# Windowed attention with two gated networks on one core: q laid out with the four head pairs innermost, and its stationary operand read with a step of 4

## The chip, the cores and the metric

The kernel runs on one core of a Trainium2 chip. The metric is the device time of one execution in microseconds. Most executions of one kernel agree within some tenths of a per cent.

## The reference

Three parts follow each other. The first is attention over 4 batches, 8 heads, 576 positions and head dimension 64, in which each query sees itself and the 63 keys before it:

```python
scores = scale * np.matmul(q, k.transpose(0, 1, 3, 2))
mask = (rel >= 0) & (rel < 64)              # rel = query position - key position
attn = softmax(np.where(mask, scores, -1e9))
x = attn @ v                                # heads side by side: (4, 576, 512)
```

The second adds to x the real part of a two-dimensional Fourier transform of x, normalises each row, and adds a network of width 2048 with a ReLU. The third is a gated network of width 1024 with a GELU, whose gate is normalised and mixed over the positions by a 576 by 576 matrix. Everything is float32 in and out.

## The kernel before, in words

**Stages.** Attention runs first, in blocks of 64 queries of all 8 heads (36 blocks: 9 in each of 4 batches). The Fourier transform and the normalisation of the first batches (`dft`, `ln`) and the decoding of the first weights (`decode_f`) are woven into it. Then come the ReLU network (`mlp`), with the rest of the transform beside it, and the gated network (`gate_u`, `v_tiles`, `spatial`, `project`). Later stages use matmuls in three terms (`mm3`, lines 113 to 120) of operands of 128 by 128 and 128 by 256 or 320.

**A block of attention.** `scores` (line 254) computes four products, one for each pair of heads, of a 128 by 128 stationary operand from q and 128 keys from k. The stationary operand of a pair has the 64 dimensions of one head on partitions 0 to 63 and those of the other on partitions 64 to 127; its 128 columns are 64 queries of the first head and 64 of the second, and the two off-diagonal quarters are zero. Each such float32 matmul is two loads of the stationary operand and two matmuls in the trace, so that 36 blocks of 4 pairs make 288 of each. VectorE adds the mask and takes the maximum (line 264), GpSimd and ScalarE make the exponential, `transposes` (line 277) turns the block by PE, `pv` multiplies by v, `norm` divides, and `xt` (line 317) turns the result into `uT`. A block's transposes come one block behind its scores, pv two behind, xt three behind (`LAG`).

**Where q lives.** Three tiles `qring` (line 196) serve as a ring; each holds two blocks. The zero quarters are written once, by 6 memsets on VectorE and 6 on GpSimd (lines 199 and 200). `load_q` (line 211) fills the other quarters: one DMA for each half of the partitions, 64 partitions each, for two blocks at a time (for one block in the first two and in the last of a batch). In the tile a partition's row is (block, head pair, half, query), so that 64 queries of a head, 256 bytes, stand together, and the other half's zeros stand between them.

**Queues.** All loads but those of the Fourier tables are issued by SP, in the order that `load_attn` (line 235) gives them: q, then k of three blocks, then v. `load_attn(n + 4)` follows the scores of block n. At the start SP issues the q and k of block 0, the mask, the q of block 1, the q of blocks 2 and 3, the v of block 0, and then the k of blocks 3 to 5. A load waits until the matmuls that read its buffer before are done, and what stands behind it on SP waits as well.

**Order of the work.** The lanes that are woven into attention advance by written costs (`drive`, line 734). A planner with its own estimates of each instruction's duration then orders the instructions of each engine; the order is fixed when the program is built.

Of the kernel before, what the change touches and what calls it, by code (L numbers as in the profile page):

```python
# [9 lines left out]
F32 = mybir.dt.float32  # L10
# [7 lines left out]
B, H, S, D = 4, 8, 576, 64  # L18
DM, FF, FG = 512, 2048, 1024
NB = S // 64  # L20
# [17 lines left out]
UB, SB, QB, VB = 3, 3, 3, 3  # L38
# [16 lines left out]
def tables():  # L55
    d = np.arange(256.0)[:, None]
    dp = np.arange(258)
    ang = 2 * np.pi * ((d * dp) % 512) / 512
    cd = np.cos(ang)
    cd[0] = 1 - dp % 2  # L60
    cd[:, 257] = 0
    sd = np.sin(ang)[:, :256]
    sd[(d[:, 0:1] * dp[:256] % 256) == 0] = 0
    t = np.arange(289.0)[:, None]
    tp = np.arange(290)
    ang = 2 * np.pi * ((t * tp) % 576) / 576
    cs = np.cos(ang)
    cs[288] *= 0.5
    cs[:, 289] = 0
    ss = np.sin(ang)  # L70
    ss[(t * tp) % 288 == 0] = 0
    ss[:, 289] = 0
    out = []
    for m in (cd, sd):
        for p in split(m):
            out.append(p.reshape(2, 128, -1).transpose(1, 0, 2).reshape(128, -1))
    g = np.zeros((128, 258), np.float32)
    g[0] = g[32] = dp % 2
    g[:, 257] = 0
    out.append(g)  # L80
    for m in (cs, ss):
        hi, lo = split(m)
        th = np.zeros((128, 3, 290), np.float32)
        th[:, 0], th[:, 1], th[:33, 2], th[64:97, 2] = hi[:128], hi[128:256], hi[256:], hi[256:]
        tl = np.zeros((128, 3, 290), np.float32)
        tl[:, 0], tl[:, 1], tl[:33, 2] = lo[:128], lo[128:256], lo[256:]
        out += [th.reshape(128, -1), tl.reshape(128, -1)]
    return np.ascontiguousarray(np.concatenate(out, 1))


def masks():
    q = np.arange(64)[:, None]
    k = np.arange(64)[None]
    m = np.zeros((2, 64, 2, 64), np.float32)
    m[:, :, 0] = np.where(k > q, 0, -8e9)
    m[:, :, 1] = np.where(k <= q, 0, -8e9)
    m0 = m.copy()
    m0[:, :, 0] = -8e9
    return np.ascontiguousarray(np.stack([m.reshape(128, 128), m0.reshape(128, 128)], 1))


class Kernel:
# [86 lines left out]
    def open_attn(self):  # L189
        nc = self.nc  # L190
        self.ap_, self.attn_es = self.pool("attn", side="right")
        p = self.ap_
        self.aps_, es = self.pool("attn_ps", side="right", space=PSUM)
        self.attn_es.enter_context(es)
        self.mask = p.tile([128, 2, 128], F32, name="mask")
        self.qring = [p.tile([128, 2, 4, 2, 64], F32, name=f"q{i}") for i in range(QB)]
        for t in self.qring:
            for i in range(2):
                nc.vector.memset(t[0:64, i, :, 1], 0.0)
                nc.gpsimd.memset(t[64:128, i, :, 0], 0.0)  # L200
        self.qt = {}
        self.kt, self.vt = {}, {}

# [7 lines left out]
    def load_q(self, b, j, w):  # L211

        t, o = self.qring[(b * 5 + j // 2) % QB], j % 2
        for h in range(2):
            dst = t[64 * h:64 * h + 64, o:o + w, :, h].rearrange("d n a q -> d (n a) q")
            self.nc.sync.dma_start(dst, self.aps["q"][b, h, :, j:j + w].rearrange("d n a q -> d (n a) q"))
        for i in range(w):
            self.qt[b, j + i] = t[:, o + i]

    def load_v(self, b, j):  # L220

# [27 lines left out]
    def attention(self):  # L249
        nc, p, ps = self.nc, self.ap_, self.aps_  # L250
# [3 lines left out]
        def scores(n):  # L254
            b, j = divmod(n, NB)
            q, k = self.qt.pop((b, j)), self.kt[b, j // 3]
            sc = ps.tile([128, 4, 128], F32, tag="sc", bufs=2, name="sc")
            for hp in range(4):
                o = 64 * (j % 3)
                nc.tensor.matmul(sc[:, hp], lhsT=q[:, hp].rearrange("p a b -> p (a b)"), rhs=k[:, hp, o:o + 128], start=True, stop=True)  # L260
            mx = p.tile([128, 4], F32, tag="mx", bufs=3, name="mx")
            s = p.tile([128, 4, 128], F32, tag="s", bufs=SB, name="s")
            for hp in range(4):
                nc.vector.tensor_tensor_reduce(
                    out=s[:, hp], in0=sc[:, hp], in1=self.mask[:, int(j == 0)], scale=1.0, scalar=-3e38,
                    op0=ALU.add, op1=ALU.max, accum_out=mx[:, hp:hp + 1])
            if n % XP[0] >= XP[1]:
                nc.gpsimd.tensor_tensor(out=s, in0=s, in1=mx[:].unsqueeze(2).to_broadcast([128, 4, 128]), op=ALU.subtract)
                nc.scalar.activation(out=s, in_=s, func=AF.Exp, scale=0.125)
            else:  # L270
                nm = p.tile([128, 4], F32, tag="nm", bufs=3, name="nm")
                nc.gpsimd.tensor_scalar(out=nm, in0=mx, scalar1=-0.125, scalar2=None, op0=ALU.mult)
                for hp in range(4):
                    nc.scalar.activation(out=s[:, hp], in_=s[:, hp], func=AF.Exp, bias=nm[:, hp:hp + 1], scale=0.125)
            st[n] = s
# [61 lines left out]
        for n in range(N + LAG[2] + 1):  # L337
            if n in TAB_AT:
                self.load_tables(TAB_AT.index(n))
            if n < N:  # L340
                scores(n)
            self.load_attn(n + 4)
            if n < N:
                yield 870
            m = n - LAG[0]
            if 0 <= m < N:
                transposes(m)
                yield 440
            m = n - LAG[1]
            if 0 <= m < N and full(m):  # L350
                pv(m)
                yield 1800 if m % NB % 2 else 900
                norm(m)
            m = n - LAG[2]
            if 0 <= m < N and full(m):
                xt(m)
                yield 440
# [548 lines left out]
def layout(q, k, v, w1, w2, w_in, g, w_sg, b_sg, w_out):  # L906
    ca = np.ascontiguousarray
    ho = list(ORDER)
    o = {}
    o["q"] = ca(q[:, ho].reshape(B, 4, 2, NB, 64, D).transpose(0, 2, 5, 3, 1, 4))  # L910
    kt = np.zeros((B, 128, 4, 64 + S), np.float32)
    kt[:, :, :, 64:] = k[:, ho].reshape(B, 4, 2, S, D).transpose(0, 2, 4, 1, 3).reshape(B, 128, 4, S)
    o["k"] = kt
    vt = np.zeros((B, 64 + S, 8, 65), np.float32)
    vt[:, :, :, 64] = 1
    vv = v[:, ho].transpose(0, 2, 1, 3)
    vt[:, 64:, 0:4, 0:64] = vv[:, :, 0:4]
    vt[:, 64:, 4:8, 0:64] = vv[:, :, 4:8, ::-1]
    o["v"] = vt.reshape(B, 64 + S, 520)
    w = lambda a: ca(a).view(np.int64)  # L920
    o["w1"] = w(w1[SIGMA].reshape(4, 128, NF, 128).transpose(2, 1, 0, 3)).reshape(NF, 128, 512)
    o["w2"] = w(w2[:, SIGMA]).reshape(NF, 128, 512)
    o["wi"] = w(w_in[SIGMA].reshape(4, 128, 2, 512).transpose(2, 0, 1, 3)).reshape(8, 128, 512)
    o["wo"] = w(w_out[:, SIGMA]).reshape(4, 128, 512)
    st = w_sg.T
    o["sg"] = ca(np.concatenate([st[:256], st[320:], st[256:320], st[256:320]]).reshape(5, 128, S))
    o["g"] = ca(g.reshape(4, 128).T)
    o["b"] = ca(b_sg.reshape(1, S))
    o["tab"] = tables()
    o["mask"] = masks()  # L930
    return o
# [20 lines left out]
```

## Time and profile before

| | |
|---|---|
| median of three runs | 819.7 us (814.97 to 820.48) |
| the profiled execution | 818.62 us, of which the span of its instructions is 816.9 us |
| TensorE (PE) busy | 785.6 us, 96% of the span |
| VectorE (DVE) busy | 486.1 us, 60% |
| ScalarE (ACT) busy | 278.0 us, 34% |
| GpSimd (POOL) busy | 194.6 us, 24% |
| DMA packets | 59322, of which 22384 under 512 bytes |
| granted TensorE clock, mean | 0.99 |

PE stands for matmuls and PEld for the loads of their stationary operands, which go on beside matmuls. Busy time is the time in which at least one instruction of the engine is under way. A matmul's duration contains its way through the array, so that consecutive ones overlap in time; the pace of a group is read from its whole length and its count. DMA is the busy share of the core's 16 DMA engines. [...]

### The profile page before, as it was taken

How to read it: one execution, taken by the hardware profiler on the slowest of the kernel's cores; microseconds unless marked ns; L12 is line 12 of the kernel's file. 1: busy time of each engine (PE TensorE's matmuls, PEld its weight loads, DVE VectorE, ACT ScalarE, POOL GpSimd, SP SyncE). 2: the span in 40 equal slices, each digit the busy share in tenths (PEclk: the TensorE clock that was granted, in tenths of full speed). 3: DMA queues.
4: the chain of work that ended last, by engine and by line, in shares of the span. 5: the costliest groups of instructions: out<-in, count | busy, mean ns of one | idle time of the engine just before them, and what ended most of it. 6: DMA issues, size and time to landing. Idle time of an engine off the chain costs nothing. (4 is left out here: it accounts for less than half of the span.)

```text
span 816.9 us, 15597 instructions
## 1 busy us (share of the span) xinstructions
PE 785.6 (96%) x6084; PEld 754.2 (92%) x6084; DVE 486.1 (60%) x1390; ACT 278.0 (34%) x638; POOL 194.6 (24%) x238
## 2 busy tenths in 40 slices
PE   7979789899999999999999999999999999999998
PEld 6869678799998999999999999999999998989898
DVE  3678988997478547972235933653240267565753
ACT  2655565443233224431113411333233243131310
POOL 3464746343032003420002300232251020010000
PEclk9989999999999999999999999999999999999999
DMA  8996641122002002430001400122131010303032
GB/s 232 307 274 188 172 136 44 39 92 78 1 28 78 1 1 79 130 104 1 1 1 53 130 26 1 33 89 94 59 103 42 1 53 8 117 1 117 1 116 93
DMA packets 59322, 63.71 MB, mean 78 GB/s; under 512 B 22384, under 2 KB 42736, under 8 KB 59248
## 3 DMA queue, kind: packets, MB, share of 16 engines
q1 hardware_dynamic: 58672, 59.75, 25.2%
q0 software_dynamic: 576, 2.97, 1.2%
q8 instruction: 48, 0.79, 0.4%
q14 instruction: 26, 0.21, 0.1%
HBM read 53.25 MB, written 9.44 MB: 77 GB/s over the span
## 5 line engine op out<-in xcount | busy, mean ns | idle before, releaser
L118 PE MATMUL acc<-rh,set 128*128 128x256 f32 (+1 forms) x512 | 151.5, 296 | 2.3 <-DVE uT L555 2.2
L118 PE MATMUL h<-xh,set 128*128 128x256 f32 (+1 forms) x512 | 151.2, 296 | 1.2 <-DVE rl L575 1.2
L119 PE MATMUL acc<-rl,set 128*128 128x256 f32 (+1 forms) x512 | 151.3, 296 | 0.0
L120 PE MATMUL acc<-rh,set 128*128 128x256 f32 (+1 forms) x512 | 151.1, 295 | 0.0
L119 PE MATMUL h<-xl,set 128*128 128x256 f32 (+1 forms) x512 | 151.0, 295 | 0.0
L120 PE MATMUL h<-xh,set 128*128 128x256 f32 (+1 forms) x512 | 150.9, 295 | 0.0
L160 POOL TENSOR_TENSOR set<-dec_w,set 128x256 fp32r<-128x256 f32 x88 | 70.8, 810 | 242.4 <-ACT set L159 238.9
L575 DVE SCALAR_TENSOR_TENSOR rl<-h,rh 128x320 fp32r<-128x320 f32 (+1 forms) x128 | 58.1, 454 | 118.1 <-ACT rh L574 117.5
L574 ACT ACTIVATE rh<-h 128x320 fp32r<-128x320 f32 (+1 forms) x128 | 51.8, 405 | 160.7 <-PE h L120 120.9
L118 PEld LDWEIGHTS acc<-rh,set 128*128 128x128 f32 x512 | 96.4, 188 | 3.9 <-issue 2.3
L118 PEld LDWEIGHTS h<-xh,set 128*128 128x128 f32 x512 | 96.3, 188 | 2.1 <-DVE rl L575 1.8
L120 PEld LDWEIGHTS acc<-rh,set 128*128 128x128 f32 x512 | 96.5, 188 | 0.1
L119 PEld LDWEIGHTS h<-xl,set 128*128 128x128 f32 x512 | 96.4, 188 | 0.1
L120 PEld LDWEIGHTS h<-xh,set 128*128 128x128 f32 x512 | 96.4, 188 | 0.0
L119 PEld LDWEIGHTS acc<-rl,set 128*128 128x128 f32 x512 | 96.4, 188 | 0.0
L555 DVE TENSOR_TENSOR uT<-acc,uT 128x320 f32<-128x320 f32 (+1 forms) x160 | 62.0, 447 | 15.1 <-PE acc L120 15.1
L154 ACT ACTIVATE dec_g<-dec_s 128x256 f32<-128x256 f32 x88 | 38.5, 439 | 76.4 <-DVE dec_w L156 38.8
L488 POOL TENSOR_TENSOR rq<-rq,mhalf 128x1 f32<-128x1 f32 (+2 forms) x26 | 17.4, 670 | 187.5 <-DVE rq L487 184.4
L155 DVE TENSOR_SCALAR dec_w<-dec_s 128x256 int32<-128x256 int32 x88 | 37.4, 428 | 34.6 <-POOL set L160 23.1
L120 PE MATMUL c<-xh,set 128*128 128x256 f32 (+1 forms) x188 | 55.4, 294 | 0.0
L118 PE MATMUL c<-xh,set 128*128 128x256 f32 (+1 forms) x188 | 55.3, 294 | 0.0
L119 PE MATMUL c<-xl,set 128*128 128x256 f32 (+1 forms) x188 | 55.3, 294 | 0.0
(193 smaller groups left out, 1639.6 us busy)
## 6 DMA issues: line engine op xcount, KB each, us to landing
dec_s<-in_w SPq DMA_DIRECT2D x64, 256.0 KB, 2.8
v<-in_v SPq DMA_DIRECT2D x16, 520.0 KB, 5.1
k<-in_k SPq DMA_DIRECT2D x11, 512.0 KB, 7.1
dec_s<-in_wi SPq DMA_DIRECT2D x16, 256.0 KB, 2.7
q<-in_q SPq DMA_DIRECT2D x30, 128.0 KB, 6.1
x<-uT SPq DMA_DIRECT2D x4, 640.0 KB, 3.9
out<-uT SPq DMA_DIRECT2D x4, 640.0 KB, 3.9
dec_s<-in_wo SPq DMA_DIRECT2D x8, 256.0 KB, 2.6
```

Source lines behind the costliest of these rows:

```text
L118: mm(out, lhsT=lh, rhs=rh, start=first and i == 0, stop=False)
L119: mm(out, lhsT=lh, rhs=rl, start=False, stop=False)
L120: mm(out, lhsT=ll, rhs=rh, start=False, stop=last and i == n - 1)
L154: nc.scalar.activation(out=g, in_=s[:, :, 1].bitcast(F32), func=AF.Copy, scale=2.0 ** -112)
L155: nc.vector.tensor_scalar(out=w, in0=s[:, :, 0], scalar1=29, scalar2=None, op0=ALU.logical_shift_right)
L160: (eng or nc.gpsimd).tensor_tensor(out=lo[:, o:o + 256], in0=f, in1=hi[:, o:o + 256], op=ALU.subtract)
L488: self.nc.gpsimd.tensor_tensor(out=y, in0=v, in1=self.mhalf[:m, 0:n], op=ALU.pow)
L555: V.tensor_tensor(out=x, in0=acc[:, c, 0:size], in1=x, op=ALU.add)
L574: A.activation(out=rh, in_=o, func=AF.Relu)
L575: V.scalar_tensor_tensor(out=rl, in0=o, scalar=0.0, in1=rh, op0=ALU.max, op1=ALU.subtract)
```

## The change

The array q in device memory has its last two axes exchanged, so that query comes before head pair. In the tile a partition's row becomes (block, half, query, head pair). A block's data for one partition are then 256 consecutive floats, 1 KB, where there were four runs of 256 bytes. The load moves the same bytes with that shape. The zero quarters become one run of 1 KB for each block, and one memset covers both blocks of a tile: 3 memsets on each engine of twice the size. The stationary operand of head pair `hp` is now every fourth float of the block, from the float `hp` on.

```diff
-        self.qring = [p.tile([128, 2, 4, 2, 64], F32, name=f"q{i}") for i in range(QB)]
+        self.qring = [p.tile([128, 2, 2, 64, 4], F32, name=f"q{i}") for i in range(QB)]
         for t in self.qring:
-            for i in range(2):
-                nc.vector.memset(t[0:64, i, :, 1], 0.0)
-                nc.gpsimd.memset(t[64:128, i, :, 0], 0.0)
+            nc.vector.memset(t[0:64, :, 1], 0.0)
+            nc.gpsimd.memset(t[64:128, :, 0], 0.0)
...
-            dst = t[64 * h:64 * h + 64, o:o + w, :, h].rearrange("d n a q -> d (n a) q")
-            self.nc.sync.dma_start(dst, self.aps["q"][b, h, :, j:j + w].rearrange("d n a q -> d (n a) q"))
+            dst = t[64 * h:64 * h + 64, o:o + w, h].rearrange("d n q a -> d n (q a)")
+            self.nc.sync.dma_start(dst, self.aps["q"][b, h, :, j:j + w].rearrange("d n q a -> d n (q a)"))
         for i in range(w):
-            self.qt[b, j + i] = t[:, o + i]
+            self.qt[b, j + i] = t[:, o + i].rearrange("p h q a -> p (h q) a")
...
-                nc.tensor.matmul(sc[:, hp], lhsT=q[:, hp].rearrange("p a b -> p (a b)"), rhs=k[:, hp, o:o + 128], start=True, stop=True)
+                nc.tensor.matmul(sc[:, hp], lhsT=q[:, :, hp], rhs=k[:, hp, o:o + 128], start=True, stop=True)
...
-    o["q"] = ca(q[:, ho].reshape(B, 4, 2, NB, 64, D).transpose(0, 2, 5, 3, 1, 4))
+    o["q"] = ca(q[:, ho].reshape(B, 4, 2, NB, 64, D).transpose(0, 2, 5, 3, 4, 1))
```

## Rows read from the trace of the kernel before

**Rows 1.** Busy time by stretch: stretch, length, busy us (instructions) of each engine, clock, DMA.
```profile
0.00:20.00 20.00, 14.74 (x97) 13.40 (x98) 6.29 (x46) 5.96 (x13) 7.24 (x23) 0.91 0.88 228
20.00:40.00 20.00, 19.16 (x226) 16.37 (x225) 13.86 (x82) 13.46 (x30) 9.53 (x16) 1.00 1.12 304
40.00:60.00 20.00, 14.77 (x141) 12.61 (x140) 16.21 (x54) 11.10 (x27) 12.95 (x14) 0.83 1.09 282
60.00:140.00 80.00, 70.91 (x724) 62.80 (x723) 69.37 (x260) 45.93 (x107) 44.40 (x51) 0.96 0.50 141
140.00:816.90 676.90, 666.00 (x4906) 648.99 (x4906) 380.35 (x951) 201.60 (x462) 120.51 (x137) 1.00 0.17 53
```

**Rows 2.** What PE waited for, 0 to 60 us: total us, times, longest.
```profile
PE xt L323 <- DVE x L313: 3.3, 1, 3.3
PE sc L260 <- DMA k<-in_k: 2.3, 1, 2.3
...
PE pv L294 <- DMA v<-in_v: 1.2, 1, 1.2
PE sc L260 <- DMA q<-in_q: 0.8, 1, 0.8
```

**Rows 3.** PE in order of time, first 20 us: start, length, instruction, count, idle before.
```profile
5.73 3.30 PE L260 MATMUL sc<-k,q 128*128 128x128 f32 x16
9.81 1.13 PE L260 MATMUL sc<-k,q 128*128 128x128 f32 x8 [0.79 <-DMA q<-in_q]
...
13.69 1.13 PE L260 MATMUL sc<-k,q 128*128 128x128 f32 x8 [2.31 <-DMA k<-in_k]
```

**Rows 4.** DMA queues in three stretches (112.6 to 114.2, 572 to 574, 0 to 60).
```profile
q1 hardware_dynamic: 544, 0.13, 36.3%
...
q1 hardware_dynamic: 375, 0.38, 56.0%
...
q1 hardware_dynamic: 19792, 13.31, 86.0%
q0 software_dynamic: 555, 2.88, 16.5%
...
q<-in_q SPq DMA_DIRECT2D x18, 128.0 KB, 7.9
...
q<-in_q SPq DMA_DIRECT2D x8, 64.0 KB, 5.1
```

**Rows 5.** SP's time to issue one load, minimum/median/maximum in ns, by tile.
```profile
L216 SPq DMA_DIRECT2D q<-in_q x42: 595/622/2002, 0.7 to 111.9; - x42
...
L208 SPq DMA_DIRECT2D k<-in_k x13: 564/630/2329, 2.3 to 96.6; - x13
...
L233 SPq DMA_DIRECT2D v<-in_v x16: 368/485/2815, 6.9 to 127.5; - x16
...
L151 SPq DMA_DIRECT2D dec_s<-in_w x16: 328/407/743, 18.5 to 147.2; - x16
```

**Rows 6.** Instructions by line and shape, 0 to 180 us: busy us, mean ns of one.
```profile
L260 PEld LDWEIGHTS sc<-k,q 128*128 128x128 f32 x288 | 37.9, 207 | 6.6 <-POOL s L268 2.5 <-DVE mx L264 2.2 <-POOL nm L272 0.9
...
L154 ACT ACTIVATE dec_g<-dec_s 128x256 f32<-128x256 f32 x22 | 9.5, 436 | 11.0 <-DVE dec_w L156 8.4 <-DMA dec_s<-in_w 2.5
L159 ACT ACTIVATE set<-dec_w 128x256 fp32r<-128x256 f32 x20 | 8.1, 409 | 4.0 <-DVE dec_w L157 3.8
L118 PEld LDWEIGHTS h<-xh,set 128*128 128x128 f32 x30 | 5.7, 189 | 0.7 <-DVE rl L575 0.7
...
L199 DVE MEMSET q<- 64x256 f32 x6 | 1.6, 272 | 0.9 <-PEq L939 0.8
...
L323 PEld LDWEIGHTS xt<-ident,x 64*128 64x128 f32 x16 | 1.4, 137 | 0.8 <-issue 0.3 <-DVE mx L264 0.2 <-ACT uT L325 0.2
...
L118 PEld LDWEIGHTS g<-tab,eh 128*33 128x33 f32 x6 | 0.7, 109 | 0.0
```

**Rows 7.** One block's scores in order of time, matmuls and loads, at full clock.
```profile
61.84 1.05 PE L260 MATMUL sc<-k,q 128*128 128x128 f32 x8
...
61.73 0.98 PEld L260 LDWEIGHTS sc<-k,q 128*128 128x128 f32 x8
```

## The prediction

> **What bounds the kernel now.** I read the busy time by stretch first. From 140 us on PE works 666.0 of 676.9 us [rows 1]; the change touches nothing there, so what it gains or loses before 140 us arrives at the end as it is. Up to 140 us PE is busy 14.74 + 19.16 + 14.77 + 70.91 = 119.6 us and idle 20.4 us. That idle time is what faster loads can win, and also what can swallow longer work of PE. The list of waits says who causes it in the first 60 us: the DMAs of k, v and q together 2.3 + 1.2 + 0.8 = 4.3 us, VectorE 3.3 us at once [rows 2]. The order in time shows where: the scores of block 3 start at 13.69 us, after 2.31 us of waiting for k, those of block 2 wait 0.79 us for q [rows 3]. In the same stretch the two data queues take 86.0% and 16.5% of the 16 DMA engines [rows 4]: they have no room left, so shorter transfers there can start others sooner. After 60 us DMA is at 0.50 [rows 1], and a shorter transfer buys little.
>
> **The transfers.** In 112.6 to 114.2 us only packets of q were moving: 544 packets took 36.3% of 16 x 1.6 us, which is 17.1 ns for 256 bytes. In 572 to 574 us there were only packets of 1 KB: 375 took 56.0% of 16 x 2 us, 47.8 ns [rows 4]. So 1 KB of q costs 4 x 17.1 = 68.3 ns now and 47.8 ns afterwards, 20.5 ns less. By 60 us the loads of q are 18 x 128 + 8 x 64 = 2816 KB [rows 4]: 2816 x 20.5 / 16 = 3.6 us less on each DMA engine, in the stretch where they are full. All 36 blocks are 4608 KB, 5.9 us, of which the last 2.3 us fall where DMA has room and are worth nothing.
>
> **The issues.** A load of q for two blocks has 64 x 8 = 512 runs and takes SP 622 ns; k, with 128 x 4 = 512 runs, takes 630; v with 256 runs at least 368; the packed weights with 128 runs at least 328, median 407 [rows 5]. So runs set the time, and q with 64 x 2 = 128 runs should take 330 to 410, some 0.25 us less. There are 42 such loads, 10 us of SP. Nearly all of that lies beside PE's work, except at the start: six loads of q are issued ahead of the k for which PE waits at 13.69 us. It is issued 6 x 0.25 = 1.5 us sooner, and 512 KB of q ahead of it move 512 x 20.5 / 16 = 0.7 us faster. The wait of 2.31 us shrinks by up to 2.2; I take 2.0. Of the waits for v and q, 2.0 us, I take half. Both ends of this step: nothing, where the next wait (ScalarE's or VectorE's) stands right behind the DMA's, and 4.3 us from the waits. [...]
>
> **The memsets.** VectorE's 6 of 256 elements at 272 ns become 3 of 512, at about twice the time: 1.6 us either way [rows 6]. They lie before the first scores at 5.73 us [rows 3], as GpSimd's do. Nothing; if they were late, the first scores would be late by one memset, 0.5 us.
>
> **Waits and order.** Each load writes the same blocks after the same readers, so no wait is added on SP. The planner may put instructions in another order, since its loads got shorter; one slip costs or gives at most what one wait did, 3.3 us [rows 2], either way. I take 0.
>
> **The stationary operand.** This is the dear step, and no row shows a read with a step of 4. First its cover. A block's 8 loads and 8 matmuls keep a pace of about (1.05 - 0.275) / 7 = 0.111 us, 0.275 us being one matmul's way through the array; the loads' (0.98 - 0.19) / 7 = 0.113 says the same [rows 7]. How much of it does a load fill? A load of 33 columns takes 109 ns, one of 128 takes 189 [rows 6]: 0.84 ns a column and 81 ns that do not depend on it. So 128 columns fill 108 ns of the 111. There is no cover: what a load gets longer, the pair gets longer, 288 times. Then how fast can the read be? The load in front of a transpose of x takes 137 ns for 128 columns, 56 without the constant part: 0.44 ns a column, contiguous float32 too, on 64 rows [rows 6]. The read side therefore delivers twice what the scores' loads ask of it. Lower end: a column of its own 16 bytes costs no more than 0.84 ns, and the step is free. Upper end: such a column costs what four neighbours cost there, 4 x 0.44 = 1.74 ns; 128 of them are 223 ns, 115 more than 108, and 288 x 0.115 = 33.1 us more on PE. A gain is excluded, since the matmuls alone keep the pace of 0.111. Nearest to a stepped read is ScalarE's read with a step of 2, 436 ns against 409 for the contiguous one of the same size [rows 6]: 7% more, and 7% of 108 would be 8 ns, 2 us in all. With the read side at half its rate I take the lower end, 0, and keep both.
>
> [...]
>
> **The sum.** -2.0 (k) - 1.0 (v, q) + 0 (memsets, order, operand) = -3.0 us. The profiled execution took 818.6 us (span 816.9), 1.1 below the median of the runs: 815.6 on the one, 816.7 on the other. I say **816 us**. Its own range is 811 to 820: the larger gain at one end, no gain and a slip in the order at the other.
>
> **Rivals.**
>
> 1. *The stepped load becomes PE's pace.* Place: line 260. Price: up to 33.1 us of PE. For it: no cover [rows 6, 7]. Against it: the read side's spare rate. PE then has 119.6 + 33.1 us of work up to what was 140 us, and half of its 20.4 us of idle time would swallow some of it: 33.1 - 10.2 - 3.0 = +20, **838 us**. With all of the idle time used 826 to 829, with none 849 to 852. It decides from the point where it overcomes the gain and 1%: 3 + 8.2 = 11.2 us, 39 ns a load where nothing is swallowed, some 75 ns where half is.
> 2. *The loads were the bound of the first 60 us.* All 4.3 us of the waits go, and 3.5 of the 5.2 us of the low clock: 818.6 - 7.8 = **811 us**, or 809 with a favourable order. For it: the full DMA queues. Against it: the waits on DMA are only 4.3 us of the 11.3 that PE stands idle up to 60 us.
> 3. *Nothing arrives.* q lands sooner, but k and v, issued behind their buffers, and VectorE set the pace: **818.6 us**, give or take an order slip. For it: VectorE is busy 69.4 of 80 us from 60 to 140 [rows 1].
>
> **How the numbers follow.** Forecast 0.36, first rival 0.39, second 0.13, third 0.12. The first rival is about as likely as the forecast alone, but the cases with a free load hold 0.61 together and lie side by side, so the forecast stays among them. A difference under 1% (8.2 us) cannot be told from none here. Faster by more: most of the second rival and a little of the forecast, 0.13. Slower by more: the first rival, 0.39, as its lowest time is 826 and a part of a slowdown stays under the bound only in few cases. Within 1%: 0.48. The range leaves out less than 0.1 at either end: 811 to 842.
>
> **What would show it.** Right: packets under 512 bytes fall by 18432 - the 36 blocks' 128 x 4 runs - from 22384 to about 4000; SP's issue of q takes 330 to 410 ns; the scores of block 3 start about 2 us sooner; a block's 8 loads still take 0.98 us and their mean stays near 207 ns. Wrong by the first rival: these loads take about 320 ns, the 8 matmuls 1.85 us instead of 1.05, and PE's busy time grows by up to 33 us, all before 160 us. Wrong by the third: the load's rows are as forecast, and the waits on k and v are as long as before or go to VectorE.

## The result, and the profile after

The changed kernel takes 828.55 us (median of 6 runs, 827.42 to 829.62), the kernel before 818.43 us beside it (6 runs, 814.97 to 820.48): a ratio of 1.0126 [1.0108, 1.0143], 10 us slower. The forecast was 816; 828.5 lies between it and the 838 of the first rival. The profiled execution took 829.62 us, its span is 827.8 us.

The busy time by stretch of the changed kernel, with the columns of [rows 1]:

```profile
0.00:20.00 20.00, 15.90 (x70) 15.31 (x71) 5.74 (x40) 6.18 (x13) 6.29 (x19) 0.91 0.85 233
20.00:40.00 20.00, 20.00 (x179) 18.82 (x179) 11.95 (x66) 10.10 (x24) 8.01 (x13) 1.00 1.09 298
40.00:60.00 20.00, 19.96 (x194) 18.31 (x193) 13.34 (x53) 10.78 (x25) 9.66 (x12) 1.00 0.94 275
60.00:140.00 80.00, 75.65 (x634) 69.52 (x634) 61.51 (x246) 43.86 (x103) 40.20 (x46) 0.98 0.45 134
140.00:827.80 687.80, 677.52 (x5012) 660.39 (x5011) 388.13 (x986) 207.00 (x476) 128.60 (x146) 1.00 0.17 54
```

Read the counts beside the busy time. From 20 to 60 us PE is busy for 39.96 us, where it was for 33.93 [rows 1], and gets through hardly more matmuls: 179 + 194 = 373 against 226 + 141 = 367. From 60 to 140 us it is 634 in 75.65 us against 724 in 70.91. PE stands idle 8.5 us up to 140 us in place of 20.4, and it is late all the same.

The reason is in the instructions by line up to 180 us, which answer to [rows 6]; the columns are busy us and mean ns of one:

```profile
L259 PE MATMUL sc<-k,q 128*128 128x128 f32 x288 | 73.8, 402 | 2.6 <-DMA k<-in_k 2.0 <-DVE mx L263 0.6
L259 PEld LDWEIGHTS sc<-k,q 128*128 128x128 f32 x288 | 69.9, 327 | 3.6 <-issue 2.2 <-DVE mx L263 0.8
...
L198 DVE MEMSET q<- 64x512 f32 x3 | 1.5, 485 | 1.0 <-PEq L938 0.9
L199 POOL MEMSET q<- 64x512 f32 x3 | 1.4, 519 | 0.1
```

The load of a pair's stationary operand takes 327 ns, where it took 207, and the loads' busy time went from 37.9 to 69.9 us. A block's scores in order of time, matmuls first and then loads, answer to [rows 7]:

```profile
87.44 2.03 PE L259 MATMUL sc<-k,q 128*128 128x128 f32 x8
...
87.33 1.94 PEld L259 LDWEIGHTS sc<-k,q 128*128 128x128 f32 x8
```

Eight loads fill 1.94 us in place of 0.98, and the eight matmuls, which follow at the loads' pace, 2.03 in place of 1.05.

What PE waited for up to 60 us, against [rows 2], and the first scores in order of time, against [rows 3]:

```profile
PE g L331 <- POOL ident masks.py:199: 2.1, 1, 2.1
PE sc L259 <- DMA k<-in_k: 2.0, 1, 2.0
```

```profile
5.53 5.85 PE L259 MATMUL sc<-k,q 128*128 128x128 f32 x24
...
13.77 2.18 PE L259 MATMUL sc<-k,q 128*128 128x128 f32 x8 [1.96 <-DMA k<-in_k]
```

The waits for v and q are gone and VectorE's 3.3 us too; the one for k has 0.3 us less, and the scores of block 3 start at 13.77 us, as before (13.69).

The transfers of 0 to 60 us (packets, then the share of SP's queue), against [rows 4], and SP's issue of q (minimum/median/maximum), against [rows 5]:

```profile
DMA packets 11700, 16.14 MB, mean 269 GB/s; under 512 B 875, under 2 KB 8254, under 8 KB 11695
...
q1 hardware_dynamic: 11119, 13.10, 79.8%
```

```profile
L215 SPq DMA_DIRECT2D q<-in_q x42: 488/600/1400, 0.7 to 119.4; - x42
```

The queue's share fell from 86.0 to 79.8%, 3.7 us of each engine's 60. Some 0.6 us of that, at the 47.8 ns of a packet of 1 KB [rows 4], are 0.21 MB that had not moved yet by 60 us (13.10 MB for 13.31). The issue of q is hardly shorter: 600 for 622.

### The profile page after: what moved, and what is told of

It is laid out like the page before. It is cut to its first block, busy times and chain, and to the rows that moved or that the text cites. A ratio compares the mean times of both kernels' runs of the same rounds, so it can differ in the third digit from the quotient of the medians.

```text
span 827.8 us, 15592 instructions
## 1 busy us (share of the span) xinstructions
PE 809.0 (98%) x6084; PEld 782.4 (95%) x6084; DVE 480.7 (58%) x1387; ACT 277.9 (34%) x638; POOL 192.8 (23%) x235
## 2 busy tenths in 40 slices
DMA packets 45498, 63.71 MB, mean 77 GB/s; under 512 B 3952, under 2 KB 28912, under 8 KB 45424
## 4 chain that ended last, share of the span: by engine, by line
PE 83%; DVE 8%; DMA 3%; ACT 2%; issue 2%; SPq 1%; POOL 1%; DVEq 0%; ACTq 0%
PE sc L259 7%; PE acc L118 7%; PE acc L119 7%; PE acc L120 7%; PE h L120 6%; PE h L119 6%; PE h L118 6%; PE c L119 6%; PE c L118 6%; PE c L120 6%; PE g L118 3%; PE g L119 3%; PE g L120 3%; PE pv L293 3%; PE pt L280 2%; DMA dec_s<-in_wo 2%
## 5 line engine op out<-in xcount | busy, mean ns | idle before, releaser
L160 POOL TENSOR_TENSOR set<-dec_w,set 128x256 fp32r<-128x256 f32 x88 | 68.9, 790 | 246.7 <-ACT set L159 246.5
L259 PE MATMUL sc<-k,q 128*128 128x128 f32 x288 | 73.8, 402 | 2.6 <-DMA k<-in_k 2.0
L259 PEld LDWEIGHTS sc<-k,q 128*128 128x128 f32 x288 | 69.9, 327 | 3.6 <-issue 2.2
```

Source lines behind the costliest of these rows:

```text
L160: (eng or nc.gpsimd).tensor_tensor(out=lo[:, o:o + 256], in0=f, in1=hi[:, o:o + 256], op=ALU.subtract)
L259: nc.tensor.matmul(sc[:, hp], lhsT=q[:, :, hp], rhs=k[:, hp, o:o + 128], start=True, stop=True)
```

## The experiments

**1. The step alone.** The loads, the layout and the order of every engine's work are those before; only the stationary operand is read at a step of 4.

```diff
-lhsT=q[:, hp].rearrange("p a b -> p (a b)")
+lhsT=q.rearrange("p a b c -> p (a b c)")[:, hp:hp + 509:4]
```

> Loads, layout and the order of all engines as in the kernel before; only the stationary operand of the scores is read with a step of 4 (so other columns of q are multiplied than the reference asks for). Theory A (the step alone makes each load 120 ns longer, PE's idle time and the low clock in the first 140 us swallow two thirds): loads of the scores at 327 ns as in the changed kernel, PE busy time on them 73 us, total 828 to 834 us. Theory B (the longer load comes from the step, but the new order of work is what swallowed 22 of the 32 us): loads at 327 ns, total 838 us or more. Theory C (the loads are longer because the new layout or its DMAs disturb them): loads near 207 ns, total 818 us.

836.93 us against 819.75: 1.0217 [1.0185, 1.0248], 17 us, between the times of theories A and B. The loads of the stationary operand, in this kernel, and two of its groups of scores in order of time:

```profile
L260 PEld LDWEIGHTS sc<-k,q x288: 307/329/332, 5.6 to 156.2; 128*128 128x128 f32 x144
...
72.42 2.02 PE L260 MATMUL sc<-k,q 128*128 128x128 f32 x8
...
89.50 2.96 PE L260 MATMUL sc<-k,q 128*128 128x128 f32 x12
```

The pace of a pair of load and matmul is (2.96 - 2.02) / 4 = 0.235 us, where it was 0.111 [rows 7]. Theory C is out, since the load is long with the old layout and the old DMAs. The step alone makes the whole slowdown and more. How much of it is swallowed shows up to the first matmul of the ReLU network, which comes at 154.1 us before and at 173.1 us here; from there to the end the two spans differ by 1.2 us (662.8 and 661.6). The row of the kernel before, then that of this one, with the columns of [rows 1]:

```profile
0.00:154.10 154.10, 130.77 (x1306) 114.33 (x1307) 117.43 (x468) 82.84 (x188) 78.63 (x110) 0.94 0.68 183
```

```profile
0.00:173.10 173.10, 160.29 (x1306) 145.28 (x1306) 118.43 (x468) 83.14 (x188) 78.27 (x110) 0.96 0.59 163
```

PE has the same 1306 matmuls and is busy 29.5 us longer; it is idle 12.8 us in place of 23.3. So 29.5 - 10.5 = 19.0 us arrive there.

**2. The loads alone.** The layout, the 1-KB runs and the order of work are those of the changed kernel; the stationary operand is a contiguous stretch of the block.

```diff
-lhsT=q[:, :, hp]
+lhsT=q.rearrange("p q a -> p (q a)")[:, 192 + 16 * hp:320 + 16 * hp]
```

> Layout, DMAs with runs of 1 KB and the order of all engines as in the changed kernel; only the stationary operand is 128 neighbouring floats across both halves (other columns than the reference asks for). Theory A (the step alone costs): loads at 207 ns, total 814 to 819 us, a gain of 0 to 4 us from the shorter transfers, the wait for k of block 3 still about 2 us. Theory B (the new order matters): the total is 4 us or more away from the kernel before, on either side, at an unchanged load. Theory C (layout or DMAs disturb the load): loads near 327 ns, 828 us.

811.32 us: 0.9896 [0.9862, 0.9931] of the kernel before, 8.4 us faster, and under the 814 to 819 us of theory A: at an unchanged load, it is what theory B said of the order. The load of the stationary operand is back at its old length:

```profile
L260 PEld LDWEIGHTS sc<-k,q x288: 186/192/338, 5.5 to 131.5; 128*128 128x128 f32 x144
```

The stretch up to the ReLU network's first matmul, in this kernel and then in the changed one, which differ in the step alone:

```profile
0.00:147.50 147.50, 125.72 (x1306) 111.74 (x1307) 109.70 (x465) 81.98 (x188) 78.26 (x107) 0.97 0.67 191
```

```profile
0.00:165.20 165.20, 154.55 (x1307) 142.60 (x1307) 112.65 (x465) 83.07 (x188) 77.02 (x107) 0.98 0.59 170
```

Again PE is busy 28.8 us longer with the step, and 11.1 us of idle time are gone: 17.7 us arrive. Within the noise the two parts add up: 17.2 - 8.4 = 8.8 us, and the change as a whole costs 10.1 (1.0217 x 0.9896 = 1.0111, against 1.0126 [1.0108, 1.0143]).

**3. Runs of 512 bytes, a step of 2.** Head pairs are laid two by two innermost: a run is (query, pair of two), and the stationary operand is every second float.

```diff
-self.qring = [p.tile([128, 2, 2, 64, 4], F32, name=f"q{i}") for i in range(QB)]
+self.qring = [p.tile([128, 2, 2, 2, 64, 2], F32, name=f"q{i}") for i in range(QB)]
...
-lhsT=q[:, :, hp]
+lhsT=q[:, hp // 2].rearrange("p h q a -> p (h q) a")[:, :, hp % 2]
```

> The reference's result, with two head pairs innermost: DMA runs of 512 bytes and a stationary operand read with a step of 2. If a read is slowed only where every column is 16 bytes or more from the last: loads at 207 ns, total 814 to 819 us. If each larger step costs in proportion: loads near 240 to 250 ns, PE 10 us longer on the scores, total 819 to 824 us.

811.34 us (809.78 to 816.05): 0.9908 [0.9880, 0.9937]. It is faster than both kernels, as fast as experiment 2, and under both of the times that were expected. Its order of work is the changed kernel's: in the two traces the instructions of every engine, the memsets aside, follow each other alike.

```profile
L260 PEld LDWEIGHTS sc<-k,q x288: 193/197/337, 5.7 to 135.3; 128*128 128x128 f32 x144
```

A step of 2 costs 5 ns a load (197 against 192, the medians). Packets under 512 bytes number 3952, as in the changed kernel.

**4. The step for half of the pairs.** Order and loads of before; a step of 4 for the first two head pairs of each block only.

```diff
-lhsT=q[:, hp].rearrange("p a b -> p (a b)")
+lhsT=q.rearrange("p a b c -> p (a b c)")[:, hp:hp + 509:4] if hp < 2 else q[:, hp].rearrange("p a b -> p (a b)")
```

> As the kernel before, in the same order, but two of the four head pairs are read with a step of 4 (other columns of q). 144 loads longer by 120 ns, 16 us more of PE on the scores. If idle time swallows first and only what is left arrives: 0 to 3 us over the kernel before. If a fixed third arrives: 5 us over it, 823 to 824 us.

825.71 us: 1.0080 [1.0049, 1.0111], 6 us, or 4 to 9 with the interval. That idle time swallows first, so that 0 to 3 us arrive, is out. Half of the 17.2 us of the whole step would be 8.6, which the interval does not exclude. The stretch up to the ReLU network's first matmul:

```profile
0.00:162.50 162.50, 142.89 (x1305) 127.58 (x1306) 118.15 (x468) 83.12 (x188) 77.41 (x110) 0.97 0.65 173
```

PE is busy 12.1 us longer than in the kernel before and idle 3.7 us less (19.6 in place of 23.3): a third of the longer work is swallowed, as in experiment 1 (10.5 of 29.5 us). That the first part of it would find more idle time than the rest is not shown.

**5. and 6. Loads and order taken apart.** The planner, which saw other loads, had put the work in another order. Experiment 5 has the loads of before with the order of experiment 3, experiment 6 the loads of experiment 3 with the order of before; the other order is written out by an edge from each instruction to the next on its engine.

```diff
+for name, last in zip(written[1:], written):   # one such list for each engine
+    tc.add_manual_dep(have[name], last, info, reason="written order")
```

> Loads, layout and operands of the kernel before (runs of 256 bytes, contiguous operand), but every engine's instructions in the order that the planner gave the kernel with runs of 512 bytes. Theory T (the 8 us that the longer runs gave back come from faster transfers): total 816 to 821 us, as the kernel before. Theory P (they come from the order that the planner wrote once it took the loads for shorter): total 809 to 814 us. Each of the two a half: 814 to 817.

> The reverse: runs of 512 bytes and an operand with a step of 2, in the order of the kernel before. Theory T: total 809 to 814 us, as with its own order. Theory P: total 816 to 821 us, as the kernel before, although no packet of q is under 512 bytes.

| | order before | order of experiment 3 |
|---|---|---|
| loads before | 1 | 0.9956 [0.9930, 0.9981] (815.48 us) |
| 512-byte runs | 0.9991 [0.9966, 1.0016] (817.28 us) | 0.9908 [0.9880, 0.9937] (811.34 us) |

Each ratio is to the kernel before, measured beside it. Faster transfers alone give nothing that can be measured. The order alone gives 0.4%, and with the faster transfers 0.8%. That it gives more with them is not clear of the noise: the two alone would make 0.9956 x 0.9991 = 0.9947, and each ratio is known to about 0.3%. PE's waits up to 60 us speak for it. Experiment 5, then experiment 3:

```profile
PE sc L260 <- DMA k<-in_k: 7.1, 3, 4.2
...
PE pv L294 <- DMA v<-in_v: 4.0, 1, 4.0
...
PE sc L260 <- DMA q<-in_q: 1.8, 2, 1.4
```

```profile
PE sc L260 <- DMA k<-in_k: 3.3, 1, 3.3
...
PE pv L294 <- DMA v<-in_v: 2.1, 1, 2.1
PE sc L260 <- DMA q<-in_q: 1.1, 2, 0.8
```

In the new order PE waits 12.9 us for k, v and q with the old loads and 6.5 with the new ones; in the order of before it waits 4.3 us [rows 2] and, with the new loads, 3.4 (experiment 6: 2.5 for k, 0.9 for q). So the new order seems to ask for them sooner. What the order itself gives shows less clearly. Experiments 6 and 3 differ in it alone. VectorE's decoding of weights by line up to 150 us (busy us, mean ns of one), and then the stretch up to the ReLU network, of experiment 6:

```profile
L156 DVE SCALAR_TENSOR_TENSOR dec_w<-dec_g,dec_w 128x256 int32<-128x256 int32 x12 | 9.7, 804 | 0.0
```

```profile
0.00:153.10 153.10, 131.70 (x1307) 115.26 (x1307) 117.75 (x468) 82.62 (x188) 78.33 (x110) 0.96 0.63 184
```

The same two of experiment 3:

```profile
L156 DVE SCALAR_TENSOR_TENSOR dec_w<-dec_g,dec_w 128x256 int32<-128x256 int32 x12 | 7.4, 619 | 0.3
```

```profile
0.00:151.10 151.10, 129.94 (x1306) 115.67 (x1307) 109.70 (x468) 82.00 (x188) 78.65 (x110) 0.94 0.67 186
```

VectorE does the same 468 instructions in 8 us less. This comes with the order and not with the loads, as experiment 5 has it too:

```profile
0.00:153.90 153.90, 127.14 (x1305) 112.54 (x1306) 109.97 (x468) 81.73 (x188) 78.67 (x110) 0.96 0.70 183
```

Which wait of PE this shortens no run isolates. A part of the gain may also be the clock: in experiment 2 PE is busy 5.0 us less than before with the same 1306 matmuls, at a granted clock of 0.97 against 0.94. The lower level of the clock is 0.50 in these traces (97 to 100 us of the kernel before, in the next section), so that this is 2 x 0.03 x 147.5 = 8.9 us at the lower level against 18.5. Half of the difference, 4.8 us, is an estimate of what it cost: a contiguous block's matmuls took 1.91 us at 0.50 and 1.05 at 1.00. The profiled executions of experiments 3 and 5 were the longest of their kernels (816.05 and 818.8 us), so these rows may understate what the medians show. This part stays open.

**7. and 8. A step of 3, a step of 8.** Loads and order of before for step 3; for step 8 the planner's order differs a little. One run each.

```diff
-lhsT=q[:, hp].rearrange("p a b -> p (a b)")
+lhsT=q.rearrange("p a b c -> p (a b c)")[:, hp:hp + 382:3]          # step 3
+lhsT=q[:].rearrange("p n a b c -> p (n a b c)")[:, hp:hp + 1017:8]  # step 8, over two blocks
```

> As the kernel before, in the same order, with the stationary operand read with a step of 3 (other columns of q), 12 bytes: 4 columns in 3 stretches of 16 bytes. If a read is slowed for every new stretch of 16 bytes that gets fewer than two of them: loads of 280 to 300 ns, between step 2 (197) and step 4 (329). If only a step of 16 bytes or more is slow: loads of 192 to 200 ns.

> As the kernel before, with a step of 8, 32 bytes, across both blocks of the tile (other columns of q). If one access to each stretch of 16 bytes is the price: loads of 327 to 330 ns, as with a step of 4, total 832 to 840 us. If the price grows with the distance: loads well over 330 ns.

They took 827.36 and 833.87 us. The loads at step 3 with two groups of scores in order of time, then the loads at step 8:

```profile
L260 PEld LDWEIGHTS sc<-k,q x288: 251/262/337, 5.7 to 145.1; 128*128 128x128 f32 x144
...
72.16 1.55 PE L260 MATMUL sc<-k,q 128*128 128x128 f32 x8
...
81.90 2.26 PE L260 MATMUL sc<-k,q 128*128 128x128 f32 x12
```

```profile
L260 PEld LDWEIGHTS sc<-k,q x288: 312/335/343, 7.8 to 151.1; 128*128 128x128 f32 x144
```

At a step of 3 the load took 262 ns, which neither theory had (280 to 300, or 192 to 200). A count of stretches fits it. 128 floats at a step of 2, 3, 4 touch 64, 96 and 128 stretches of 16 bytes, and of each load the 81 ns that do not depend on the columns, an estimate of the prediction [rows 6], are taken off first: (197 - 81) / 64 = 1.81, (262 - 81) / 96 = 1.89, (329 - 81) / 128 = 1.94 ns a stretch. The pace says the same without the 81 ns: (2.26 - 1.55) / 4 = 0.178 us at a step of 3 and 0.235 at 4 (experiment 1) are 1.85 and 1.84 ns a stretch. At a step of 8 there are 128 stretches too, and the load is hardly longer than at 4 (335 ns for 329, or 1.98 ns a stretch). So at these steps of 2 to 8 the load's time went by the number of stretches touched, not by their distance. A contiguous load touches 32, and its 108 ns for 128 columns, 0.84 ns each, is more than the 62 that they would cost at 1.94.

**9. The changed kernel in the order of before.** Its loads and its step, with the order written out as in experiment 6 (and its memsets split as before).

```diff
+    tc.add_manual_dep(have[name], last, info, reason="written order")
```

> The loads of the changed kernel (1-KB runs) and its step of 4, with the order of work of the kernel before written out by hand on every engine. Theory A (the 8 us that loads and order give back come by the new order; shorter transfers alone give nothing): step 4 costs its 17 us, loads give 0, so about 836 us, as the step alone did, and 1.021 of the kernel before. Theory B (the shorter transfers give the gain by themselves, whatever the order): 828 us, as the changed kernel, 1.012.

838.47 us: 1.0252 [1.0217, 1.0287], against 1.0217 [1.0185, 1.0248] for the step alone and 1.0126 for the changed kernel. With the old order the faster transfers give nothing here either. Loads and step are the same in both, so what softened the change from 838 to 828.5 us is the order of work. Up to the ReLU network, to set beside the changed kernel's row under experiment 2:

```profile
0.00:173.70 173.70, 160.02 (x1307) 145.06 (x1307) 118.52 (x468) 83.17 (x188) 78.47 (x110) 0.96 0.56 162
```

PE is busy 5.5 us longer than in the changed kernel and idle 3.0 us longer. A part of the busy time is the clock, granted at 0.96 against 0.98: 2 x 0.04 x 173.7 = 13.9 us at the lower level against 6.6, and half of the difference, up to 3.6 us, is lost by the estimate of experiments 5 and 6.

**10. The same step on the moving side.** The kernel before, in its order, with q contiguous and k read at a step of 4. One run.

```diff
-rhs=k[:, hp, o:o + 128]
+rhs=k[:].rearrange("p a b -> p (a b)")[:, hp + o:hp + o + 509:4]
```

> The kernel before, its order of work too, with the stationary q contiguous as before and the moving k of the scores read with a step of 4 elements (the columns are other ones than the reference's, so the scores are other numbers). Theory A (any operand of TensorE read at a step of 4 costs some 1.9 ns for each 16-byte stretch): a matmul of 128 columns takes about 240 ns in place of 111, the pace of a pair as the step on the stationary side gave, and the time is about 836 us. Theory B (the cost is the weight load's, and the moving side has slack at this step): the pace stays near 111 ns and the time near 819 us.

835.79 us, nearly that of experiment 1. Loads by line, and two groups of scores in order of time:

```profile
L260 PEld LDWEIGHTS sc<-k,q x288: 186/208/337, 6.6 to 155.6; 128*128 128x128 f32 x144
```

```profile
72.43 1.98 PE L260 MATMUL sc<-k,q 128*128 128x128 f32 x8
...
89.42 2.88 PE L260 MATMUL sc<-k,q 128*128 128x128 f32 x12
```

The single load stays near its old length (208 ns for 192), but eight matmuls take 1.98 us, where they took 1.05 [rows 7]: the moving side pays nearly the same. A pair's pace is (2.88 - 1.98) / 4 = 0.225 us here and 0.235 with the step on the stationary side (experiment 1).

## Why the prediction was wrong, point by point

**The stationary operand: the failed step.** "With the read side at half its rate I take the lower end, 0". The upper end was the right one. It said 115 ns a load and 33.1 us of PE; the load's mean grew by 120 (207 to 327), and experiment 1 has it by itself: the row of the line, the matmuls' busy time, grew there from 41.7 to 73.5 us, by 31.8.

That the size fits so well is in part luck. At full clock the load grew by 137 ns (192 to 329, the medians) and the pace by 0.235 - 0.111 = 0.124 us. Where the clock was low the step cost far less, which the forecast did not consider. The granted clock of a stretch and a block's matmuls in it, before and then in the changed kernel:

```profile
97.00:100.00 3.00, 3.00 (x14) 2.78 (x14) 3.00 (x17) 2.25 (x5) 2.43 (x1) 0.50 0.84 197
...
97.88 1.91 PE L260 MATMUL sc<-k,q 128*128 128x128 f32 x8
```

```profile
16.00:19.00 3.00, 3.00 (x14) 2.88 (x15) 0.93 (x8) 1.28 (x4) 0.22 (x1) 0.50 1.14 305
...
16.29 2.23 PE L259 MATMUL sc<-k,q 128*128 128x128 f32 x8
```

At 0.50, the lower level throughout, eight matmuls take 1.91 us contiguous and 2.23 at a step of 4, 0.32 us more; at 1.00 they take 1.05 [rows 7] and 2.03, 0.98 more. PE had stood idle for 1.74 us just ahead of the first of these stretches, and for 1.96 us some 2 us ahead of the second. So a contiguous pair was at the lower level nearly as slow as a pair with a step of 4: 1.91 us for eight, against 2.23 there and 2.03 at 1.00.

The fault lay in how the row of the transpose's load was used: 0.44 ns a column, contiguous [rows 6], was read as spare rate for any column. But counted by stretches of 16 bytes, four floats each, that rate is 1.74 ns a stretch. Experiments 1, 3 and 7 gave 1.8 to 1.9 ns for each stretch touched, close to that 1.74: in experiment 1 a load that used one float of four took 1.94. In experiment 8 twice the distance added 6 ns a load (335 for 329). The row held the price; ScalarE's step of 2, a neighbour by its looks, held two floats to a stretch and could not show it.

Beside the contiguous load of 192 ns, two floats to a stretch cost 5 ns (197, experiment 3) and one to a stretch 137 (329, experiment 1).

**The cover and what swallows it.** "There is no cover" held: loads and pairs lengthened together. The first rival's sum was 33.1 of work less 10.2 of idle time; measured were 28.8 to 29.5 us of busy time less 10.5 to 11.1. In experiment 1 PE as a whole grew by 2 us less than the row of the line. The clock can account for them: it was granted at 0.94 up to 154.1 us before and at 0.96 up to 173.1 us there, which is 18.5 and 13.8 us at the lower level, and half of the difference, by the same estimate, is 2.3 us. With the wrong end for the step went the chances: the rival that held 0.39 was the mechanism. Its 838 us came out where the order was kept (experiment 9, 838.47), but by luck: PE's work grew there by 29.3 us and not by 33.1, idle time swallowed 9.7 of it, and the 3.0 us that the loads were to give did not come.

**The order: "I take 0".** This is the second term that was off. It gave about 10 us between experiment 9 and the changed kernel, outside the 3.3 us that one slip was given. The forecast looked for a wait moved here or there; the planner put all engines' work in another sequence from its own durations.

**The transfers.** 3.6 us less on each engine was forecast, 3.7 came (86.0 to 79.8%, some 0.6 of it since less had moved), and the packets under 512 bytes are 3952 of the forecast 4000. What this was to win, 2.0 us at k and 1.0 at v and q, did not follow from the transfers: with the order kept, experiment 6 (runs of 512 bytes) is within 0.9966 to 1.0016, and experiment 9 (1 KB) is no faster than experiment 1. The scores of block 3, which wait for k, still start at 13.77 us in the changed kernel. SP's issue of this k in order of time, and the queue from 5 to 14 us, before and then in the changed kernel:

```profile
7.57 0.57 SPq L208 DMA_DIRECT2D k<-in_k  x1
...
q1 hardware_dynamic: 4246, 2.37, 100.0%
```

```profile
7.15 0.57 SPq L207 DMA_DIRECT2D k<-in_k  x1
...
q1 hardware_dynamic: 2148, 2.32, 95.5%
```

It was issued 0.4 us sooner, where 1.5 was forecast, and landed no sooner (13.64 us for 13.56). With half of the packets the queue moved as much in that stretch and was nearly as full; why the shorter transfers did not bring k sooner, these runs do not settle.

**The issues.** 330 to 410 ns was forecast for q, 600 came, with a quarter of the runs. So it is not the number of runs that sets SP's time for this load; what does stays open. PE's waits for q are gone from the changed kernel all the same.

**The memsets.** 485 and 519 ns, three on each engine: about as forecast, and the first scores start no later (5.53 us for 5.73).

**Rivals two and three.** The loads as the bound (811 us): the time of experiments 2 and 3, but it came with the new order, and the faster transfers alone did not give it. Its 5.2 us of the low clock are an estimate like that of experiments 5 and 6, half of the 3.6 and 6.8 us at 0.50 that 0.91 up to 20 us and 0.83 from 40 to 60 us make [rows 1]. No run shows them as a gain: the changed kernel was granted 0.91 and 1.00 there, and experiment 2 came to an estimated 4.8 us up to the ReLU network. Nothing arrives (818.6 us): true of the transfers alone (experiment 6).

## What to carry to other kernels

A read of TensorE's operand with a step cost here by the 16-byte stretches that it touched, 1.8 to 2.0 ns each at steps of 2 to 8. A layout could interleave float32 by two for longer runs of DMA at 5 ns a load (197 for 192); a step of 3 took a pair of load and matmul that has no cover from 0.111 to 0.178 us, a step of 4 to 0.235, at full clock. The rate of the transpose's contiguous load was here close to a rate of stretches (1.74 ns each); price an operation that uses a part of each by them before any row that merely resembles it. Where a planner orders the work, a changed transfer can act through the order alone, as in experiment 5 (0.9956 [0.9930, 0.9981]); keep the order fixed in one experiment before the gain is put down to the transfer.

## What was not expected of the hardware

The moving side had hardly more slack than the stationary one at a step of 4: 0.225 us a pair (experiment 10) and 0.235 (experiment 1), where contiguous operands took 0.111. And the same VectorE instruction, `dec_w` of 128 by 256, takes 379 ns at best, 420 in the median and up to 2842 in experiment 6. There the longest stands beside an addition of GpSimd, in order of time:

```profile
84.55 2.84 POOL L395 TENSOR_TENSOR O<-uT 128x1152 f32<-128x1152 f32 x1
84.83 2.84 DVE L156 SCALAR_TENSOR_TENSOR dec_w<-dec_g,dec_w 128x256 int32<-128x256 int32 x1
```

The same two stand side by side in the kernel before (85.77 and 86.04 us), where this instruction takes up to 2842 ns as well. In the changed kernel, with the new order, they do not, and the longest is 1446 ns, there and in experiment 3. So this is one place where the order acts on VectorE, worth some 2.4 of its 8 us; that the addition is the cause was not tried by itself.
